# Joining the two words of a 64-bit weight on VectorE instead of ScalarE and GpSimd

## The chip, the cores and the metric

The kernel runs on one core of one Trainium2 chip. A core has five engines, each with its own instruction queue: TensorE (PE in the profile; its weight loads are shown apart as PEld), VectorE (DVE), ScalarE (ACT), GpSimd (POOL) and SyncE (SP), which here issues most of the transfers. Work on different engines is ordered by semaphores only. The metric is the time of one execution on the device, in microseconds (us). Before the change its median is 1007.48 us (three runs, 1007.32 to 1007.81).

## The reference

Attention with a causal window and a linear position bias, then a bilinear feed-forward layer:

```
q, k, v: (8, 8, 576, 64) float32
w_a, w_b: (512, 1536) float64;  w_out: (1536, 512) float64

scores = q @ k^T / 8 - slope[h] * |i - j|    where 0 <= i - j < 128, else -1e9
x      = softmax(scores) @ v                 -> (4608, 512)
out    = ((x @ w_a) * (x @ w_b)) @ w_out     -> (4608, 512)
```

The weights arrive as 64-bit floating-point numbers. The kernel has to turn them into 32-bit ones itself, and then into pairs of 16-bit ones (a high and a low part), since the products run in float16 with three terms each.

## The kernel before, in words

There are eight batches. For each, an attention stage makes x (512 rows by 576 tokens), an "up" stage makes the product of two projections (1536 rows, in 12 blocks f), and a "down" stage multiplies it with w_out. While PE works on one batch's up and down stages, the attention of the next batch runs beside it in small steps.

The weights are prepared once, beside batch 0. `up_weights` goes through 12 blocks of w_a and w_b, `down_weights` through 6 pairs of blocks of w_out: 18 conversions in all, each of 128 x 1024 values that lie as pairs of 32-bit words (low, high) in a buffer which is a part of the tile `wdn`. Three such buffers take turns. The result, float32, goes to a part of the tile `wup`. One conversion (`convert`) is:

- L131, DVE: the high word shifted left by 3 and masked: the exponent's low bits and the upper 20 bits of the mantissa at their float32 place.
- L133, DVE: the two top bits of the high word (sign and exponent) joined to it.
- L130, ACT: the low word, read as an unsigned number, times 2^-29, written back as an integer: the 3 mantissa bits that are still missing.
- L135, POOL, twice (each for 512 of the 1024): that number added.

Behind it ACT squares the converted block into a free place (L141), PE sums the squares with a matrix of ones (L156, tile `wn_ps`; for w_out an accumulated sum and, at the end, L101), DVE takes the largest (L161), POOL makes a power of two from it (L107, L111, L114), and with that scale ACT (L149) writes the float16 high part and DVE (L150) the low part into `wup`. For w_out this last step is L230 and L231, into `wdn`.

The attention of batch 0 (`first_attention`) is the first thing that PE does. For each of four head pairs and four banks of scores PE makes products (L569, `sc_ps`), DVE adds the bias and takes the minimum (L580, `mn`), ACT the exponential (L581), PE transposes (L587), DVE or ACT copies (L592 to L595), and at the end of a pair PE multiplies with v (L501, `x_ps`) and DVE scales (L619). Steps of the weights are put between: `other(0.5)` twice per bank. Then comes batch 0's up stage (L836, tile `up_ps`, evacuated by ACT at L783 and DVE at L785, split into float16 parts at L829 and L830, the latter on DVE for the first six blocks and on POOL for the last six), with batch 1's attention beside it (L374, L382, L383, L399, L400, L296), and its down stage (L812).

What sets the order: SP's queue is in the order of the code throughout, and PE's from batch 1 on. All other queues, and PE's through batch 0, are ordered at build time by a scheduler that works with its own durations. The loads of weights (L119) stand in SP's queue: the load for conversion n+3 is issued behind the sum of squares of conversion n. In SP's queue before the load for the ninth conversion stands the load of v for batch 1 (L268).

Of the kernel before, what the change touches and what calls it, by code (L numbers as in the profile page):

```python
# [15 lines left out]
U32 = mybir.dt.uint32  # L16
I64 = mybir.dt.int64
AF = mybir.ActivationFunctionType
ALU = mybir.AluOpType
# [27 lines left out]
def attention_then_bilinear_ffn(ctx: ExitStack, tc: tile.TileContext, qT, kT, vP, w_a, w_b, w_out, rel, slopes2, outT):  # L47
    nc = tc.nc
    vec, act, pe, pool, sp = nc.vector, nc.scalar, nc.tensor, nc.gpsimd, nc.sync
# [71 lines left out]
    def words(n):  # L121

        w = raws[n % 3].bitcast(I32).rearrange("p m (n two) -> p m n two", two=2)
        return w[:, :, :, 0], w[:, :, :, 1], forms[n % len(forms)].bitcast(I32)

    def convert(n):

        low, high, t = words(n)

        act.activation(low, low.bitcast(U32), AF.Copy, scale=float(2.0**-29))  # L130
        vec.tensor_scalar(out=t, in0=high, scalar1=3, scalar2=0x3FFFFFF8, op0=ALU.logical_shift_left, op1=ALU.bitwise_and)  # L131
        yield
        vec.scalar_tensor_tensor(out=t, in0=high, scalar=-0x40000000, in1=t, op0=ALU.bitwise_and, op1=ALU.bitwise_or)  # L133
        for m in range(2):
            pool.tensor_tensor(out=t[:, m, :], in0=t[:, m, :], in1=low[:, m, :], op=ALU.add)  # L135
        yield

    def squares(n, **kw):
# [26 lines left out]
    def up_weights():  # L165
# [3 lines left out]
        sq, rest, hi, ps = {}, [], [], None  # L169
        for f in range(NF + 2):  # L170
            conv = convert(f) if f < NF else iter(())
            next(conv, None)
            n = f - 1
# [30 lines left out]
    def down_weights():  # L204

        sums = small.tile([P, NF // 2], F32, tag="wos", name="wos", bufs=1)
        for n in range(NF // 2 + 1):
            conv = convert(NF + n) if n < NF // 2 else iter(())
            next(conv, None)
            yield  # L210
            next(conv, None)
            if n:
                squares(NF + n - 1, accum_out=sums[:, n - 1:n])
                if n + 2 < NF // 2:
                    load_weights(NF + n + 2, (w_out[2 * n + 4], w_out[2 * n + 5]), sp)
            yield
        sab = small.tile([P, NF], F32, tag="sab", name="sab", bufs=1)
        vec.tensor_tensor(out=sab, in0=sup[:, :, 0], in1=sup[:, :, 1], op=ALU.mult)
        vec.tensor_reduce(out=smin, in_=sab, op=ALU.min, axis=AX)
        vec.reciprocal(sab, sab)  # L220
        s1 = small.tile([P, 1], F32, tag="wo1", name="wo1", bufs=1)
        vec.tensor_reduce(out=s1, in_=sums, op=ALU.add, axis=AX)
        tot = ps_at.tile([P, 512], F32, tag="at", name="wtot")
        total(tot[:, 0:1], s1)
        power_scale(so, tot[:, 0:1], 1.01, 15)
        vec.tensor_scalar(out=ratio, in0=sab, scalar1=smin, scalar2=so, op0=ALU.mult, op1=ALU.mult)
        yield
        for f in range(NF):
            s, x = ratio[:, f:f + 1], forms[f // 2][:, f % 2, :]
            act.activation(wdn[:, f, 0, :], x, AF.Copy, scale=s)  # L230
            vec.scalar_tensor_tensor(out=wdn[:, f, 1, :], in0=x, scalar=s, in1=wdn[:, f, 0, :], op0=ALU.mult, op1=ALU.subtract)  # L231
            yield
# [828 lines left out]
```

## Time and profile before

| | us |
|---|---|
| median of three runs | 1007.48 |
| span of the profiled execution, first to last instruction | 1005.2 |
| PE busy | 970.8 (97%) |
| DVE busy | 674.8 (67%) |
| ACT busy | 648.9 (65%) |
| POOL busy | 306.1 (30%) |
| L130, 18 on ACT | 20.9 |
| L131, 18 on DVE | 15.9 |
| L133, 18 on DVE | 24.1 |
| L135, 36 on POOL | 54.6 |

The profile is one execution; of it the span is known, which begins with the first instruction of the program and ends with the last, and the run's own time lies a little above it, as the median of the runs does (2.3 us). Busy time is time in which an engine executes; a matmul's end is modelled, so a busy PE is not PE at its peak. In a group's row the figure behind the bar is its busy time, the next the mean duration in ns, and then follows how long the engine was idle just before these instructions and what ended that. All 18 conversions lie in the first 153 us.

### The profile page before, as it was taken

How to read it: one execution, taken by the hardware profiler on the slowest of the kernel's cores; microseconds unless marked ns; L12 is line 12 of the kernel's file. 1: busy time of each engine (PE TensorE's matmuls, PEld its weight loads, DVE VectorE, ACT ScalarE, POOL GpSimd, SP SyncE). 2: the span in 40 equal slices, each digit the busy share in tenths (PEclk: the TensorE clock that was granted, in tenths of full speed). 3: DMA queues.
4: the chain of work that ended last, by engine and by line, in shares of the span. 5: the costliest groups of instructions: out<-in, count | busy, mean ns of one | idle time of the engine just before them, and what ended most of it. 6: DMA issues, size and time to landing. Idle time of an engine off the chain costs nothing.

```text
span 1005.2 us, 23888 instructions
## 1 busy us (share of the span) xinstructions
PE 970.8 (97%) x9339; PEld 753.6 (75%) x9339; DVE 674.8 (67%) x1833; ACT 648.9 (65%) x1715; POOL 306.1 (30%) x345
## 2 busy tenths in 40 slices
PE   8789989999999999999999999999999999999998
PEld 5557656777777777777787777777777777777776
DVE  5888999557878566785768687666677576524530
ACT  7976779657767756767767767677666766413321
POOL 3533463104565321352226112220223022211100
PEclk9889999999999999999999999999999999999999
DMA  9317733564444442462624642474425632210001
GB/s 349 120 43 269 231 114 74 120 166 80 100 90 100 137 90 43 97 172 71 121 52 105 172 90 46 93 178 103 84 57 107 163 67 43 49 37 7 2 13 36
DMA packets 148433, 102.83 MB, mean 102 GB/s; under 512 B 120032, under 2 KB 128352, under 8 KB 147296
## 3 DMA queue, kind: packets, MB, share of 16 engines
q1 hardware_dynamic: 138816, 91.77, 37.2%
q10 hardware_dynamic: 9504, 9.54, 2.9%
q8 instruction: 73, 1.20, 0.5%
q14 instruction: 40, 0.33, 0.1%
HBM read 48.33 MB, written 9.44 MB: 57 GB/s over the span
## 4 chain that ended last, share of the span: by engine, by line
PE 70%; DVE 10%; ACT 4%; DMA 2%; issue 1%; POOL 1%; SPq 0%; ACTq 0%; DVEq 0%
PE dn_ps L932 19%; PE ch L836 19%; PE p L836 14%; PE up_ps L836 10%; PE x_ps L501 4%; PE sc_ps L378 3%; DVE phl L400 2%; PE dn_ps L812 2%; DMA v<-in_vP 1%; DVE t L382 1%; DVE xs L436 1%; ACT t L383 1%; DVE wup L150 1%; ACT phl L399 1%; DVE wup L257 1%
## 5 line engine op out<-in xcount | busy, mean ns | idle before, releaser
L836 PEld LDWEIGHTS <-wup 128*128 128x128 f16 x4224 | 409.1, 98 | 120.8 <-issue 14.3
L932 PE MATMUL dn_ps<-h,wdn 128*128 128x288 f16 x2016 | 254.3, 286 | 0.0
L932 PEld LDWEIGHTS <-wdn 128*128 128x128 f16 x2016 | 193.9, 98 | 51.7
L836 PE MATMUL ch<-xs,wup 128*128 128x288 f16 x1536 | 221.5, 286 | 0.8 <-ACT rc L861 0.6
L836 PE MATMUL up_ps<-xs,wup 128*128 128x288 f16 x1536 | 197.7, 288 | 5.8 <-DVE rc L785 4.2
L836 PE MATMUL p<-xs,wup 128*128 128x288 f16 x1152 | 172.6, 286 | 0.0
L891 POOL TENSOR_TENSOR rc<-rc,row 128x288 f32<-128x288 f32 x64 | 62.3, 974 | 278.8 <-DVE row L889 262.9
L400 DVE SCALAR_TENSOR_TENSOR phl<-t,rin,phl 128x192 f16<-128x192 f32 (+2 forms) x252 | 109.5, 474 | 19.0 <-ACT phl L399 18.8
L383 ACT ACTIVATE t<-t,mn 128x192 f32<-128x192 f32 (+2 forms) x252 | 107.2, 427 | 23.3 <-DVE mn L382 23.0
L829 ACT CAST h<-rc 128x576 f16<-128x576 f32 x96 | 64.2, 669 | 68.2 <-DVE rc L896 37.6
L399 ACT ACTIVATE phl<-t,rin 128x192 f16<-128x192 f32 (+2 forms) x252 | 88.7, 425 | 23.0 <-DMA pT<-phl 10.9
L830 DVE TENSOR_TENSOR h<-rc,h 128x576 f16<-128x576 f32 x90 | 71.1, 790 | 32.7 <-ACT h L829 32.0
L382 DVE CUSTOM_DVE_ANT_0 t<-sc_ps,bias,neg 128x192 f32<-128x192 f32 (+2 forms) x216 | 73.7, 389 | 7.8 <-PE sc_ps L378 7.7
L135 POOL TENSOR_TENSOR wup<-wup,wdn 128x512 int32<-128x512 int32 x36 | 54.6, 1539 | 44.6 <-DVE wup L133 14.6
L937 ACT ACTIVATE row<-dn_ps,oi 128x288 f32<-128x288 f32 x56 | 27.6, 494 | 56.7 <-PE dn_ps L932 56.5
L873 ACT ACTIVATE row<-ch,g 128x288 f32<-128x288 f32 x64 | 31.8, 497 | 50.1 <-PE ch L836 50.1
L436 DVE TENSOR_TENSOR xs<-v,xs 128x576 f16<-128x576 f32 x52 | 48.7, 950 | 21.7 <-ACT xs L435 21.5
L360 POOL TENSOR_SCALAR bias<-rel_sb,ninv,sl_sb 128x192 f32<-128x192 f32 x24 | 21.3, 887 | 123.5 <-DVE mn L382 123.5
L868 DVE TENSOR_TENSOR rc<-p,rc 128x288 f32<-128x288 f32 x64 | 29.1, 454 | 44.4 <-PE p L836 35.0
L896 DVE SCALAR_TENSOR_TENSOR rc<-rc,g,ch 128x288 f32<-128x288 f32 x64 | 32.6, 510 | 23.8 <-PE ch L836 23.6
L383 ACT ACTIVATION_READ_ACCUMULATOR t<-t,mn 128x1 f32 x252 | 47.7, 189 | 0.0
L430 POOL TENSOR_TENSOR xq<-xq,sq 128x576 bf16<-128x576 bf16 x22 | 29.6, 1345 | 56.8 <-ACT sq L429 56.7
(151 smaller groups left out, 1315.6 us busy)
## 6 DMA issues: line engine op xcount, KB each, us to landing
v<-in_vP SPq DMA_DIRECT2D x8, 1280.0 KB, 6.5
out<-row ACTq DMA_DIRECT2D x60, 144.0 KB, 1.8
qk<-in_qT SPq DMA_DIRECT2D x28, 288.0 KB, 3.9
qk<-in_kT SPq DMA_DIRECT2D x28, 288.0 KB, 4.4
wdn<-in_w_a SPq DMA_DIRECT2D x12, 512.0 KB, 4.5
wdn<-in_w_b SPq DMA_DIRECT2D x12, 512.0 KB, 5.6
wdn<-in_w_out SPq DMA_DIRECT2D x12, 512.0 KB, 4.3
qst<-qkh SPq DMA_DIRECT2D x24, 144.0 KB, 2.7
```

The costliest lines, as they stand in the source:

```text
L135: pool.tensor_tensor(out=t[:, m, :], in0=t[:, m, :], in1=low[:, m, :], op=ALU.add)
L382: vec.tensor_tensor_reduce(out=t[:, c:c + w], in0=ps[:, c:c + w], in1=o.bias[:, WIN - w:WIN], scale=-0.125 if o.b == 1 else o.neg, scalar= ...
L383: act.activation(t[:, c:c + w], t[:, c:c + w], AF.Exp, bias=o.mn[:, n:n + 1], scale=-1.0, accum_out=o.sm[:, n:n + 1])
L399: act.activation(phl[:, 0, pc:pc + w], e, AF.Copy, scale=s)
L400: vec.scalar_tensor_tensor(out=phl[:, 1, pc:pc + w], in0=e, scalar=s, in1=phl[:, 0, pc:pc + w], op0=ALU.mult, op1=ALU.subtract)
L436: vec.tensor_tensor(out=xs[:, n, 1, :, :], in0=src, in1=xs[:, n, 0, :, :], op=ALU.subtract)
L501: pe.matmul(xp[oc // 512][64 * h:64 * h + 64, o0:o0 + w], vt[0:rows, c:c + 64], probs(pt, rows, blocks, h), start=(n == 0 and first), stop ...
L829: act.copy(h[:, f, :, 0, :], hid)
L830: eng.tensor_tensor(out=h[:, f, :, 1, :], in0=hid, in1=h[:, f, :, 0, :], op=ALU.subtract)
L836: pe.matmul(ps[:, 0:HT], wup[:, a[0], a[1], wi, k, :], xs[:, b, xi, k, :], start=(first and n == 0), stop=(last and n == len(ks) - 1), ski ...
L891: pool.tensor_tensor(out=x0, in0=x0, in1=mid, op=ALU.mult)
L932: pe.matmul(ps[:, 0:HT], wdn[:, f, wi, e * P:(e + 1) * P], h[:, f, t, hi, :], start=(m == 0 and n == 0), stop=(m == NF - 1 and n == 2))
```

## The change

The ACT conversion of the low word and the two POOL additions go. In their place DVE takes the low word, shifts it right by 29, so that its three top bits remain, and joins it with the rest by a bitwise or, one instruction over all 1024 values:

```diff
         low, high, t = words(n)
 
-        act.activation(low, low.bitcast(U32), AF.Copy, scale=float(2.0**-29))
         vec.tensor_scalar(out=t, in0=high, scalar1=3, scalar2=0x3FFFFFF8, op0=ALU.logical_shift_left, op1=ALU.bitwise_and)
         yield
         vec.scalar_tensor_tensor(out=t, in0=high, scalar=-0x40000000, in1=t, op0=ALU.bitwise_and, op1=ALU.bitwise_or)
-        for m in range(2):
-            pool.tensor_tensor(out=t[:, m, :], in0=t[:, m, :], in1=low[:, m, :], op=ALU.add)
+        vec.scalar_tensor_tensor(out=t.bitcast(U32), in0=low.bitcast(U32), scalar=29, in1=t.bitcast(U32), op0=ALU.logical_shift_right, op1=ALU.bitwise_or)
         yield
```

Lines behind the edit have numbers lower by two in the changed kernel; in it the shift is L130, the joining of the top bits L132 and the new join L133.

The scheduler orders the queues of batch 0 anew. The differences end with batch 0's down stage; behind it every queue is as before, and SP's is throughout. Three places show it. The first is DVE in batch 0's attention, third head pair, from behind its third bank of scores to the first of the next pair. Before:

```order
L133 SCALAR_TENSOR_TENSOR wup<-wdn,wup 128x2x512
L150 SCALAR_TENSOR_TENSOR wup<-wup,sup 128x2x256 x3
L131 TENSOR_SCALAR wup<-wdn 128x2x512
L150 SCALAR_TENSOR_TENSOR wup<-wup,sup 128x2x256
L580 ISA t,mn_546<-sc_ps,bias_331 128x192
L580 ISA mn_546 128x1
L580 ISA t,mn_546<-sc_ps,bias_331 128x192
L580 ISA mn_546 128x1
L595 COPY phl<-tr_ps 128x512
L133 SCALAR_TENSOR_TENSOR wup<-wdn,wup 128x2x512
L580 ISA t_163,mn_578<-sc_ps,bias_483 128x64
```

After (L132 is the former L133, L133 the join, L578 the former L580):

```order
L132 SCALAR_TENSOR_TENSOR wup<-wdn,wup 128x2x512
L133 SCALAR_TENSOR_TENSOR wup<-wdn,wup 128x2x512
L578 ISA t,mn_538<-sc_ps,bias_327 128x192
L578 ISA mn_538 128x1
L578 ISA t,mn_538<-sc_ps,bias_327 128x192
L578 ISA mn_538 128x1
L130 TENSOR_SCALAR wup<-wdn 128x2x512
L133 SCALAR_TENSOR_TENSOR wup<-wdn,wup 128x2x512
L593 COPY phl<-tr_ps 128x512
L132 SCALAR_TENSOR_TENSOR wup<-wdn,wup 128x2x512
L601 TENSOR_SCALAR rin_605<-sm_426 128x9
L133 SCALAR_TENSOR_TENSOR wup<-wdn,wup 128x2x512
```

The four splits of weights (L150) that stood between the third and fourth bank stand earlier now; two conversions' steps and their joins stand there and behind the fourth bank.

The second place is DVE in batch 0's up stage, around the last splits of w_a and w_b and two evacuations. Before:

```order
L785 SCALAR_TENSOR_TENSOR rc<-rc,g,up_ps 128x288
L219 TENSOR_REDUCE smin<-sab 128x1
L150 SCALAR_TENSOR_TENSOR wup<-wup,sup 128x2x256
L133 SCALAR_TENSOR_TENSOR wup<-wdn,wup 128x2x512
L150 SCALAR_TENSOR_TENSOR wup<-wup,sup 128x2x256 x2
L220 RECIPROCAL sab<-sab 128x12
L150 SCALAR_TENSOR_TENSOR wup<-wup,sup 128x2x256
L392 TENSOR_SCALAR rin<-sm 128x4
L785 SCALAR_TENSOR_TENSOR rc<-rc,g,up_ps 128x288
```

After (L148 is the former L150, L783 the former L785, L828 the former L830):

```order
L133 SCALAR_TENSOR_TENSOR wup<-wdn,wup 128x2x512
L148 SCALAR_TENSOR_TENSOR wup<-wup,sup 128x2x256 x3
L217 TENSOR_REDUCE smin<-sab 128x1
L132 SCALAR_TENSOR_TENSOR wup<-wdn,wup 128x2x512
L783 SCALAR_TENSOR_TENSOR rc<-rc,g,up_ps 128x288
L828 TENSOR_TENSOR h<-rc,h 128x2x288
L783 SCALAR_TENSOR_TENSOR rc<-rc,g,up_ps 128x288
L390 TENSOR_SCALAR rin<-sm 128x4
```

A join stands ahead of the splits, and the evacuations follow more closely on each other.

The third place is POOL at the end of the conversions. Before:

```order
L135 TENSOR_TENSOR wup<-wup,wdn 128x512 x2
L830 TENSOR_TENSOR h<-rc,h 128x2x288
L135 TENSOR_TENSOR wup<-wup,wdn 128x512 x4
L830 TENSOR_TENSOR h<-rc,h 128x2x288
L135 TENSOR_TENSOR wup<-wup,wdn 128x512 x2
L830 TENSOR_TENSOR h<-rc,h 128x2x288
```

After:

```order
L107 TENSOR_SCALAR cl<-wtop 128x4
L111 TENSOR_SCALAR r<-cl 128x4
L114 TENSOR_SCALAR sup<-r 128x4
L358 TENSOR_SCALAR bias<-rel_sb,sl_sb 128x192
L828 TENSOR_TENSOR h<-rc,h 128x2x288 x4
```

POOL keeps the scales, the biases and its share of the low parts of the hidden layer (L828), without an addition between them.

## Prediction

> **What bounds the kernel now.** I read the page's head first, then a table of stretches, then who made TensorE (PE) wait.
>
> ```profile
> PE 970.8 (97%) x9339; PEld 753.6 (75%) x9339; DVE 674.8 (67%) x1833; ACT 648.9 (65%) x1715; POOL 306.1 (30%) x345
> PEclk9889999999999999999999999999999999999999
> ```
>
> PE is busy 97% of the span, so an edit elsewhere pays only where it shortens one of PE's gaps or a spell of low clock. The table of stretches tells where those are (columns: stretch, its length, busy time of PE, PEld, DVE, ACT, POOL, then the granted clock, the DMA share and GB/s):
>
> ```profile
> 0.00:20.00 20.00, 15.68 (x172) 12.24 (x173) 9.63 (x31) 13.20 (x35) 7.06 (x25) 0.91 0.92 353
> 20.00:54.00 34.00, 26.74 (x266) 17.56 (x263) 30.84 (x87) 32.19 (x87) 17.05 (x19) 0.90 0.46 169
> 54.00:86.00 32.00, 28.07 (x262) 20.78 (x262) 24.96 (x63) 23.44 (x59) 10.44 (x16) 0.89 0.30 113
> 86.00:158.00 72.00, 63.76 (x536) 46.73 (x534) 68.55 (x128) 53.50 (x118) 40.74 (x31) 0.95 0.57 178
> 215.00:1005.20 790.20, 781.47 (x7538) 614.59 (x7537) 501.12 (x1407) 485.86 (x1311) 220.85 (x248) 1.00 0.37 85
> ```
>
> From 215 us on PE idles 8.7 us in 790, at full clock. Before 158 us it idles 23.8 us (4.3 + 7.3 + 3.9 + 8.2). All 18 weight conversions lie there: eight before 86 us, ten between 86 and 158. In the last stretch VectorE (DVE) is busy 68.55 of 72 us. It is the bound there; PE follows it. From 20 to 54 us DVE (30.84 of 34) and ACT (32.19) are both nearly full. PE's waits between 86 and 160 us, and the largest two before, agree:
>
> ```profile
> PE up_ps L836 <- DVE rc L785: 4.2, 2, 2.3
> PE wtot L101 <- ACT t L383: 1.7, 1, 1.7
> PE wn_ps L156 <- ACT wdn L141: 1.5, 1, 1.5
> PE sc_ps L374 <- DVE mn L382: 0.7, 1, 0.7
> ...
> PE sc_ps L569 <- DVE mn L580: 4.2, 2, 4.0
> PE wn_ps L156 <- DVE mn L382: 3.1, 1, 3.1
> ```
>
> Why is DVE so full? The groups of DVE and POOL from 86 to 158 us (count, busy, mean ns), with the two pieces of the timeline that explain the means, and the durations over the whole span (min/median/max):
>
> ```profile
> L150 DVE SCALAR_TENSOR_TENSOR wup<-wup,sup 128x512 f16<-128x512 f32 x11 | 14.0, 1289 | 1.0 <-ACT wup L149 1.0
> L133 DVE SCALAR_TENSOR_TENSOR wup<-wdn,wup 128x1024 int32<-128x1024 int32 x10 | 13.7, 1381 | 0.0
> L131 DVE TENSOR_SCALAR wup<-wdn 128x1024 int32<-128x1024 int32 x10 | 9.4, 938 | 0.2 <-DMA wdn<-in_w_b 0.2
> L830 DVE TENSOR_TENSOR h<-rc,h 128x576 f16<-128x576 f32 x5 | 5.8, 1157 | 1.3 <-ACT h L829 1.3
> L296 DVE SCALAR_TENSOR_TENSOR vhl<-v,sv,vhl 128x640 f16<-128x640 f32 x3 | 5.7, 1922 | 1.5 <-ACT vhl L295 1.5
> L135 POOL TENSOR_TENSOR wup<-wup,wdn 128x512 int32<-128x512 int32 x20 | 31.1, 1579 | 27.1 <-DVE wup L133 9.6 <-ACT wdn L130 8.1 <-ACT vhl L295 4.2
> ```
> ```profile
> 109.27 2.98 POOL L135 TENSOR_TENSOR wup<-wup,wdn 128x512 int32<-128x512 int32 x2 [3.72 <-ACT wdn L130]
> 109.35 3.44 DVE L150 SCALAR_TENSOR_TENSOR wup<-wup,sup 128x512 f16<-128x512 f32 x2
> ```
> ```profile
> L150 DVE SCALAR_TENSOR_TENSOR wup<-wup,sup x24: 733/746/1783, 33.7 to 131.6; 128x512 f16<-128x512 f32 x24
> L133 DVE SCALAR_TENSOR_TENSOR wup<-wdn,wup x18: 1203/1218/2206, 9.3 to 146.8; 128x1024 int32<-128x1024 int32 x18
> L131 DVE TENSOR_SCALAR wup<-wdn x18: 631/686/1778, 8.1 to 141.5; 128x1024 int32<-128x1024 int32 x18
> L130 ACT ACTIVATE wdn<-wdn x18: 1111/1157/1211, 8.1 to 140.5; 128x1024 int32<-128x1024 uint32 x18
> L830 DVE TENSOR_TENSOR h<-rc,h x6: 741/754/1841, 81.1 to 125.1; 128x576 f16<-128x576 f32 x6
> L296 DVE SCALAR_TENSOR_TENSOR vhl<-v,sv,vhl x4: 879/1908/1948, 142.7 to 170.4; 128x640 f16<-128x640 f32 x4
> ```
>
> Two L150 that take 0.75 us each elsewhere took 3.44 us together because POOL's two additions started 0.08 us earlier: each DVE operation lost about 1 us. That is the hidden price of the additions: they occupy POOL, which has time, and block DVE, which has none.
>
> **What the change adds.** One join per conversion, in the shape of L133 (128x1024, one strided and one packed int32 operand). The trace has no join; its nearest row is L133, at 1.22 us. The bounds are L131's 0.69 and L133 under POOL, 2.2; I take L133, which has the same operands. On the queue it is worth its step from start to start: L133 began at 107.00 and the L150 behind it at 108.14, so 1.14 us.
>
> ```profile
> 107.00 1.22 DVE L133 SCALAR_TENSOR_TENSOR wup<-wdn,wup 128x1024 int32<-128x1024 int32 x1
> 108.14 0.75 DVE L150 SCALAR_TENSOR_TENSOR wup<-wup,sup 128x512 f16<-128x512 f32 x1
> ```
>
> Ten joins from 86 to 158 us: +11.4. Eight before: +9.1. The join waits for no other engine, only for DVE's own L133 line before it and the load that L131 needed anyway. Queued behind it are L150, the score reductions L382 and the evacuations L785, for which PE waits.
>
> **What it removes from DVE.** Mean less median (for L296 less its minimum), times the count, from 86 to 158 us: L150 11 x 0.543 = 6.0; L133 10 x 0.163 = 1.6; L131 10 x 0.252 = 2.5; L830 5 x 0.403 = 2.0; L296 3 x 1.043 = 3.1. Sum 15.2 us. What the probability splits of L400 lose besides, I set against what POOL's own L830, which stays, will still take. Net on DVE there: 11.4 - 15.2 = **-3.8 us**. Bounds: -7 if L400's share counts too, and 0 if the remaining POOL work takes back a quarter of the 15.2.
>
> **What it removes elsewhere.** ACT loses 18 x 1.16 = 20.9 us of L130 and POOL 36 additions. In the saturated stretch ACT is busy 53.5 of 72 us, so this alone buys nothing; what counts is the chain from shift to square: join 1.2 in place of a POOL pair of 2.5 to 3.0 that often started late. The last conversion shows it:
>
> ```profile
> 146.76 1.89 DVE L133 SCALAR_TENSOR_TENSOR wup<-wdn,wup 128x1024 int32<-128x1024 int32 x1
> 149.75 2.54 POOL L135 TENSOR_TENSOR wup<-wup,wdn 128x512 int32<-128x512 int32 x2
> 152.32 1.06 ACT L141 ACTIVATE wdn<-wup 128x1024 bf16<-128x1024 f32 x1 [0.50 <-POOL wup L135]
> ```
>
> From the end of L133 (148.65) to the square 3.7 us pass; with a join it is 1.2. PE's waits on these squares, 1.7 (through the sum at L101) and 1.5, can shrink by up to 2.5 each; but DVE would then be the next to be late, so of these 3.2 us I count **-1.0** beyond the DVE sum (bounds 0 and -3.2).
>
> **Before 86 us.** The same rows there:
>
> ```profile
> L150 DVE SCALAR_TENSOR_TENSOR wup<-wup,sup 128x512 f16<-128x512 f32 x13 | 12.9, 1031 | 0.0
> L133 DVE SCALAR_TENSOR_TENSOR wup<-wdn,wup 128x1024 int32<-128x1024 int32 x6 | 8.0, 1326 | 0.0
> L131 DVE TENSOR_SCALAR wup<-wdn 128x1024 int32<-128x1024 int32 x6 | 5.1, 858 | 0.0
> ```
>
> Stalls: 13 x 0.285 + 6 x 0.108 + 6 x 0.172 = 5.4 us, less than the 9.1 of the joins: DVE gets 3.7 us more, ACT 8 x 1.16 = 9.3 less. DVE has 3.2 us idle from 20 to 54 and 7.0 from 54 to 86 to take it, and ACT, just as full, gets faster. The order fits: between the last two score banks of a head pair stand six operations now (one L133, four L150, one L131, the block behind PE's 4.0 us wait) and two after, but more joins follow behind the last bank. I count **0**, with bounds -3 and +4.
>
> **The clock.** Long gaps cost PE twice. The same kind of 28 products:
>
> ```profile
> 55.24 2.12 PE L501 MATMUL x_ps<-phl,v 128*64 128x128 f32 x28
> ...
> 65.93 1.03 PE L156 MATMUL wn_ps<-wdn,ones 128*128 128x256 bf16 x4 [3.13 <-DVE mn L382]
> 66.89 3.88 PE L501 MATMUL x_ps<-pT,v 128*64 128x128 f32 x28
> ```
>
> After 3.13 us idle they took 1.8 us more. From 86 to 158 us the clock was 0.95 of full, 3.6 us' worth; with half of the gaps gone I count **-1.2** (bounds 0 and -3.6). The Trainium skill ("TensorE: Matmul & The Clock Gate", Part 1) has a free-running window of about 3.4 us, after an idle one of which the clock halves. By it every gap below 3.4 us would be free and this term nearly 0; the trace has the slow products behind a shorter gap, so I keep the term.
>
> **Sum.** -3.8 - 1.0 + 0 - 1.2 = -6.0 us. The profiled span is 1005.2, 2.3 below the median of the runs, 1007.48; span 999.2, time **1001.5**. From 215 us on PE is the bound and the instruction order is the same, so I carry the gain to the end whole.
>
> **The rivals.**
> 1. *More than this* (0.14). The first part gains as well: ACT was as full as DVE from 20 to 54 us, and the gaps of 4.0 and 3.1 us with their cold products go. Another -3 to -8: 990 to 998. Against it: DVE's own load rises there.
> 2. *Nothing to measure* (0.18). The lock stays under another name: POOL's L830 and its small scale operations are still there, and a DVE queue packed with two-input operations holds POOL up, and so L149 and L150 behind it; or the order, made anew by the scheduler, gives the 6 us back in new gaps. 1005.5 to 1009.5.
> 3. *DVE becomes the bound of the first attention; slower* (0.20). From 20 to 54 us the new order puts six more bit operations, two more L150 and one more reduction ahead of the last score bank: 6 x 1.14 + 2 x 0.67 + 0.6 = 8.8 us. The stalls that go there are in these rows, 4.15 - 3 x 0.67 and 1.78 - 0.69, together 3.2:
>
> ```profile
> 33.67 4.15 DVE L150 SCALAR_TENSOR_TENSOR wup<-wup,sup 128x512 f16<-128x512 f32 x3
> 37.74 1.78 DVE L131 TENSOR_SCALAR wup<-wdn 128x1024 int32<-128x1024 int32 x1
> ```
>
> 30.84 + 8.8 - 3.2 = 36.4 in a stretch of 34. If DVE's 3.2 us idle stay as well, the last scores come 5.6 us late, and a gap beyond 3 us adds some 2 to 3 us of cold products: +8, against -6 behind it, +2; and if the second stretch gives nothing, +8. 1009.5 to 1015.5. It is decided where the last L580 ends: in the trace near 53.8 us; beyond about 58 the change loses.
>
> The Trainium skill ("Perfetto Trace Analysis", Optimizing Scalar/DVE Operations) advises to take work off a saturated DVE to ScalarE or GpSimd, the reverse of this change, and adds that DVE and GpSimd share a port; the stalled L150 rows bear out the second half, so I give the first no more than this chance.
>
> **Chances.** Forecast case 0.48 (998.5 to 1005); rivals as above. Faster by over 0.2% (2 us, about what a measurement here can tell from no change): 0.48 + 0.14 = 0.62; within: 0.18; slower: 0.20. The range that leaves out no more than 2 in 10 is 993 to 1012: the far ends of rivals 1 and 3 are cut.
>
> **What would show it.** Right: L150, L131 and L296 at their short durations (means near 0.75, 0.69, 0.9 us); joins at 1.2 us; PE's idle time from 86 to 158 us down from 8.2 to about 4; POOL without L135. Wrong: DVE means that stay long over L830; a last L580 well behind 54 us; or a new wait of PE on L141 behind the join. If DVE's stalls go but PE's gaps stay, the gaps were the order's and not DVE's load.

## The result, and the profile after

The changed kernel takes 1010.38 us (median of seven runs, 1008.78 to 1011.34), the kernel before beside it 1007.53 us (seven runs, 1006.31 to 1008.81). The ratio is 1.0026, with a 95% interval of 1.0016 to 1.0036: slower by 1.6 to 3.6 us, where 6 us less were forecast. The time lies in the range of the prediction, the direction does not.

The head of the changed kernel's page, and its table of stretches (length, busy time of PE, PEld, DVE, ACT, POOL, granted clock, DMA share, GB/s):

```profile
PE 970.9 (96%) x9339; PEld 752.5 (75%) x9339; DVE 669.1 (66%) x1851; ACT 630.7 (63%) x1697; POOL 258.1 (26%) x309
PEclk8989999999999999999999999999999999999999
```
```profile
0.00:20.00 20.00, 15.01 (x152) 11.98 (x154) 9.30 (x29) 11.04 (x33) 3.27 (x21) 0.83 0.89 341
20.00:54.00 34.00, 27.73 (x283) 17.13 (x283) 32.79 (x92) 26.95 (x79) 7.43 (x10) 0.95 0.49 176
54.00:86.00 32.00, 26.50 (x248) 19.12 (x248) 22.77 (x65) 19.86 (x55) 4.66 (x12) 0.89 0.20 74
86.00:158.00 72.00, 67.49 (x623) 51.37 (x621) 64.50 (x141) 46.91 (x115) 13.48 (x12) 1.00 0.63 195
158.00:215.00 57.00, 50.41 (x473) 36.47 (x471) 36.90 (x111) 37.34 (x101) 8.59 (x7) 0.97 0.47 96
215.00:1008.10 793.10, 783.78 (x7572) 616.42 (x7571) 502.86 (x1418) 488.56 (x1319) 220.70 (x248) 1.00 0.38 86
```

The row of the kernel before that the prediction's table did not have:

```profile
158.00:215.00 57.00, 55.10 (x572) 41.68 (x570) 39.70 (x123) 40.69 (x112) 9.96 (x9) 1.00 0.51 108
```

From 86 to 158 us PE is idle 4.5 us where it was 8.2, at clock 1.00 (of full speed) where it was 0.95. From 158 to 215 us it is the reverse: 6.6 us idle where it was 1.9, at 0.97 where it was 1.00. So the time was won, and lost again in the next stretch. The rows of batch 0's up products, first those of the kernel before, then those of the changed one (count, duration, start of the first and the last), show how much was won by then:

```profile
L836 PE MATMUL up_ps<-xs,wup x576: 282/286/448, 57.6 to 168.5; 128*128 128x288 f16 x192
```
```profile
L834 PE MATMUL up_ps<-xs,wup x576: 282/286/448, 61.1 to 163.0; 128*128 128x288 f16 x192
```

The first of them is 3.5 us later, the last 5.5 us earlier, so between the two PE won 9.0 us. DVE's groups in the changed kernel from 86 to 158 us:

```profile
L132 DVE SCALAR_TENSOR_TENSOR wup<-wdn,wup 128x1024 int32<-128x1024 int32 x10 | 12.7, 1269 | 0.0
L133 DVE SCALAR_TENSOR_TENSOR wup<-wdn,wup 128x1024 uint32<-128x1024 uint32 x10 | 12.2, 1215 | 0.0
L148 DVE SCALAR_TENSOR_TENSOR wup<-wup,sup 128x512 f16<-128x512 f32 x11 | 8.0, 759 | 0.4 <-ACT wup L147 0.4
L130 DVE TENSOR_SCALAR wup<-wdn 128x1024 int32<-128x1024 int32 x10 | 7.1, 717 | 0.0
L828 DVE TENSOR_TENSOR h<-rc,h 128x576 f16<-128x576 f32 x6 | 4.5, 750 | 2.1 <-ACT h L827 2.1
L294 DVE SCALAR_TENSOR_TENSOR vhl<-v,sv,vhl 128x640 f16<-128x640 f32 x3 | 2.7, 920 | 0.7 <-ACT vhl L293 0.7
```

The long means that the prediction named are short now (L148 is the former L150: 1289 to 759 ns), and the join costs 1.215 us.

Now the stretch in which it was lost: who made PE wait from 158 to 215 us, first in the kernel before, then in the changed one (total, times, longest):

```profile
PE n_ps L515 <- ACT row L822: 1.1, 1, 1.1
PE up_ps L836 <- ACT rc L783: 0.5, 1, 0.5
```
```profile
PE x_ps L499 <- DMA pT<-phl: 4.3, 2, 3.3
PE qtot L330 <- DVE both L322: 1.7, 2, 1.0
PE dn_ps L810 <- ACT row L820: 0.4, 1, 0.4
PE dn_ps L810 <- DVE row L818: 0.3, 1, 0.3
```

The new wait is for a transfer, the transpose of the probabilities pT<-phl of batch 1's attention, which is issued by SP once ACT and DVE have written all of phl (the normalisation, L397 and L398). There is one per head pair; the fourth lies here. SP's row of it before and after (start, length of the issue):

```profile
185.59 5.57 SPq L405 DMA_TRANSPOSE pT<-phl  x1
```
```profile
192.25 6.08 SPq L403 DMA_TRANSPOSE pT<-phl  x1
```

ACT's queue tells why it is 6.7 us late. Before, the pair's last four normalisations and then the squares of the next q and k, which wait for their load:

```profile
183.58 1.49 ACT L399 ACTIVATE phl<-t,rin 128x192 f16<-128x192 f32 x4 [0.45 <-DVE rin L396]
189.03 1.16 ACT L321 ACTIVATE qkl<-qk 128x1152 bf16<-128x1152 f32 x1 [3.96 <-DMA qk<-in_kT]
```

After, the same two the other way round:

```profile
188.69 1.16 ACT L319 ACTIVATE qkl<-qk 128x1152 bf16<-128x1152 f32 x1 [3.91 <-DMA qk<-in_kT]
189.76 0.19 ACT L319 ACTIVATION_READ_ACCUMULATOR qkl<-qk 128x1 f32 x1
189.85 1.48 ACT L397 ACTIVATE phl<-t,rin 128x192 f16<-128x192 f32 x4
```

The load lands within 0.4 us of the same time in both. In the changed kernel ACT sits idle 3.91 us in front of it, and behind it stand four normalisations, whose factors (`rin`) DVE had ready at 185.50 us. The transpose then also takes longer from issue to landing, 9.4 us instead of 7.6. And PE, at the end of this chain, in the changed kernel:

```profile
201.69 1.71 PE L499 MATMUL x_ps<-pT,vhl 128*64 128x128 f16 x42 [3.33 <-DMA pT<-phl]
203.34 1.14 PE L810 MATMUL dn_ps<-h,wdn 128*128 128x288 f16 x4
```

### The profile page after: what moved, and what is told of

The parts are those of the page before. It is cut to its first block, busy times and chain, and to the rows that moved or that the text cites. A ratio compares the mean times of both kernels' runs of the same rounds, so it can differ in the third digit from the quotient of the medians.

```text
span 1008.1 us, 23824 instructions
## 1 busy us (share of the span) xinstructions
PE 970.9 (96%) x9339; PEld 752.5 (75%) x9339; DVE 669.1 (66%) x1851; ACT 630.7 (63%) x1697; POOL 258.1 (26%) x309
## 4 chain that ended last, share of the span: by engine, by line
PE 69%; DVE 14%; DMA 7%; ACT 5%; issue 2%; SPq 1%; POOL 1%; ACTq 0%; DVEq 0%
PE dn_ps L930 19%; PE ch L834 18%; PE p L834 13%; PE up_ps L834 11%; PE x_ps L499 4%; PE sc_ps L376 3%; DMA pT<-phl 3%; DVE phl L398 2%; DMA qk<-in_kT 2%; DVE t L380 1%; DVE wup L133 1%; DMA v<-in_vP 1%; DVE wup L132 1%; DVE wup L148 1%; DMA qst<-qkl 1%
## 5 line engine op out<-in xcount | busy, mean ns | idle before, releaser
L834 PE MATMUL up_ps<-xs,wup 128*128 128x288 f16 x1536 | 195.5, 287 | 2.5 <-DVE wup L133 1.2
L398 DVE SCALAR_TENSOR_TENSOR phl<-t,rin,phl 128x192 f16<-128x192 f32 (+2 forms) x252 | 107.8, 467 | 27.1 <-ACT phl L397 27.0
L397 ACT ACTIVATE phl<-t,rin 128x192 f16<-128x192 f32 (+2 forms) x252 | 88.8, 425 | 34.3 <-DMA pT<-phl 21.1
L828 DVE TENSOR_TENSOR h<-rc,h 128x576 f16<-128x576 f32 x90 | 69.2, 769 | 33.6 <-ACT h L827 32.8
L499 PE MATMUL x_ps<-pT,vhl 128*64 128x128 f16 (+3 forms) x1176 | 46.2, 229 | 6.5 <-DMA pT<-phl 5.2
L499 PEld LDWEIGHTS <-vhl 128*64 128x64 f16 (+1 forms) x1176 | 42.7, 109 | 12.1 <-issue 5.8
```

The source lines that it names most:

```text
L397: act.activation(phl[:, 0, pc:pc + w], e, AF.Copy, scale=s)
L398: vec.scalar_tensor_tensor(out=phl[:, 1, pc:pc + w], in0=e, scalar=s, in1=phl[:, 0, pc:pc + w], op0=ALU.mult, op1=ALU.subtract)
L499: pe.matmul(xp[oc // 512][64 * h:64 * h + 64, o0:o0 + w], vt[0:rows, c:c + 64], probs(pt, rows, blocks, h), start=(n == 0 and first), stop ...
L828: eng.tensor_tensor(out=h[:, f, :, 1, :], in0=hid, in1=h[:, f, :, 0, :], op=ALU.subtract)
L834: pe.matmul(ps[:, 0:HT], wup[:, a[0], a[1], wi, k, :], xs[:, b, xi, k, :], start=(first and n == 0), stop=(last and n == len(ks) - 1), ski ...
```

## The experiments

In the diffs below, which are cut to the lines that matter, `tc.issue_after(x)` puts an instruction behind x in the order made at build time.

Theory A: the joins and the freed engines win some 6 us up to 158 us, and the order that the scheduler made anew loses more than that behind it, through late transposes. Rivals: B, the joins' time on DVE is what the change costs, and the order nothing; C, batch 1's transposes and loads have a fixed length and can't keep up with an earlier PE, however they are ordered; D, which came up with experiment 3, an order that helps does so whatever converts the weights. Every ratio is to the kernel before, run on the same chip in the same turn.

**1. The squares put back behind the normalisation.** In the changed kernel:

```diff
+        with tc.issue_after(last_norm[3].ins) if (b, p) == (2, 1) else ExitStack():
             act.activation(lo.bitcast(BF16), qk, AF.Square, accum_out=sums)
```

`last_norm[p]` is the last L397 of pair p. In the kernel before, the squares stand there already.

> The changed kernel with one place of ScalarE's order put back: the squares of the second q, k pair of batch 2 (which wait for its load) stand behind the last normalisation of batch 1's fourth pair, as they stand in the kernel before, not ahead of it. Theory A (the gain up to 158 us is real, and the new order behind it loses it, this transpose above all): the fourth transpose pT<-phl, issued at 192.25 us in the changed kernel, is issued near 187 us and lands near 195; the PE wait of 3.33 us at 201.69 us goes, and with it the clock dip to .66 of full speed behind it; the time falls by 3 to 4.5 us from the changed kernel's, to 1006 to 1007.5 us, ratio to the kernel before .9985 to 1.000. Rival B (the joins' load on VectorE costs the time, the order nothing): no change, ratio 1.0026. Rival C (the transposes and loads of batch 1's attention have a fixed length and cannot keep up with a PE that comes earlier, however they are ordered): the wait moves to the next transpose or load, and less than 1 us is won, ratio 1.0016 to 1.0026.

Measured: 1.0014 (1.0004 to 1.0023). That is 1.2 parts in 1000 below the changed kernel, no clear difference, and outside what theory A expected. The fourth transpose is issued at 188.87 us, 3.4 us earlier, not the 5 expected; PE is at the place earlier too and still waits 3.0 us. The edit moved other instructions as well: DVE's splits of phl (L399) now have five score reductions among them and end at 188.80 us, and the transpose takes 9.7 us to land. So the swap was not the only cause of the late transpose.

**2. The swap alone, in the kernel before.** `last_sq[0]` is the last of the squares.

```diff
+            if i == 3:
+                early = squares(5)
             if o:
-                with behind():
+                with tc.issue_after(last_sq[0].ins) if i == 3 else behind():
                     normalize(o)
...
-                nxt = squares(i + 1)
+                nxt = early if i == 4 else squares(i + 1)
```

> The kernel before, with the additions on GpSimd as they were, and the same swap made in it: the squares of the second q, k pair of batch 2 stand ahead of the last normalisation of batch 1's fourth pair on ScalarE; nothing else in any engine's order moves but the small product that follows them on VectorE. Theory A: ScalarE waits for the load until near 189 us with the normalisation behind it, the fourth transpose is issued near 191 us and not at 185.59, lands near 199, and PE, which wants it at 196.9, waits 2 to 3 us there: 1.5 to 3.5 us slower, ratio 1.0015 to 1.0035, with no join in the kernel. Rival B: nothing, ratio within .0005 of 1. Rival C: PE is not early in this kernel, so the transpose has slack: under 1 us, ratio below 1.001.

Measured: 1.0058 (1.0046 to 1.0070), twice what was expected. No join is in this kernel, and by the trace one instruction moved on ACT (with the read of its sum) and one on DVE, every other queue being as before; so rival B's "the order costs nothing" has fallen. The transpose is issued at 191.03 us. PE before, and then here:

```profile
196.86 1.63 PE L501 MATMUL x_ps<-pT,vhl 128*64 128x128 f16 x42
198.42 3.12 PE L812 MATMUL dn_ps<-h,wdn 128*128 128x288 f16 x24
```
```profile
200.74 2.91 PE L501 MATMUL x_ps<-pT,vhl 128*64 128x128 f16 x42 [3.29 <-DMA pT<-phl]
203.58 4.53 PE L815 MATMUL dn_ps<-h,wdn 128*128 128x288 f16 x24
```

The wait is 3.29 us, a little over the 2 to 3 expected; the same 66 products then take 7.44 us, not 4.75. The low clock behind the wait, which the expectation had left out, is 2.7 of the 5.8 us.

**3. The third transpose too.** Its normalisation stood, in the changed kernel, behind four splits of w_out and three exponentials:

```profile
166.81 2.56 ACT L228 ACTIVATE wdn<-wup,ratio 128x512 f16<-128x512 f32 x4
...
170.71 0.79 ACT L397 ACTIVATE phl<-t,rin 128x192 f16<-128x192 f32 x2
```

Experiment 1's edit, and beside it:

```diff
+            with tc.issue_after(last_norm[2].ins) if f >= 8 else ExitStack():
                 act.activation(wdn[:, f, 0, :], x, AF.Copy, scale=s)
```

> The first of these kernels, and beside that the last four splits of the output weights (f from 8) put behind the normalisation of batch 1's third pair on ScalarE. Theory A: the third transpose, issued at 174.04 us in the changed kernel, is issued about 2 us earlier, and the PE wait of .94 us at 180.89 goes: .5 to 1.5 us below the first of these kernels. Against it: the last splits come later, and the first down products, which read them in order, may wait up to 2 us for them. Rivals B and C: no difference to the changed kernel of more than 1 us.

Measured: 0.9958 (0.9946 to 0.9970), 6.8 parts in 1000 below the changed kernel where 3.5 to 6 were expected of both edits together. ACT now, and the stretch:

```profile
167.65 0.81 ACT L399 ACTIVATE phl<-t,rin 128x192 f16<-128x192 f32 x2
168.35 1.33 ACT L229 ACTIVATE wdn<-wup,ratio 128x512 f16<-128x512 f32 x2
```
```profile
158.00:215.00 57.00, 52.86 (x523) 39.50 (x521) 40.73 (x136) 40.58 (x114) 7.51 (x7) 1.00 0.57 123
```

The third transpose is issued 4.5 us earlier (169.57 us), the fourth at 183.05, because phl must be free of one before it can be written for the next: ACT's first write for the fourth pair waits for the third transpose, in the changed kernel and here:

```profile
180.86 1.68 ACT L397 ACTIVATE phl<-t,rin 128x64 f16<-128x64 f32 x5 [4.17 <-DMA pT<-phl]
```
```profile
176.38 1.68 ACT L399 ACTIVATE phl<-t,rin 128x64 f16<-128x64 f32 x5 [0.85 <-DMA pT<-phl]
```

The long PE wait is gone and the clock is 1.00. Both edits seem to be needed: the squares back alone (experiment 1) won nothing clear, and with the splits late but the squares first (experiment 8) nothing is won either. No run has the edit of the splits alone.

**4. No joins at all.** The line of the join is taken out of the changed kernel; all 18 go (the ten of the expectation are those from 86 us on), and this kernel leaves out the low three bits of each weight.

> The changed kernel without the ten joins on VectorE: the low three bits of each weight are left out, so VectorE loses 18 operations of 1.22 us (22 us), and GpSimd has no additions either; the order behind is the scheduler's for this case. Rival B (the joins' time on VectorE is what the change costs): at least 3 us below the changed kernel, 1007 us or less. Theory A: PE is 1 to 6 us further ahead at 158 us, since 12 of the 22 us lie in 86 to 158 us, where VectorE is the busiest engine of the two that feed PE; its order in 158 to 215 us still has squares ahead of the fourth pair's normalisation, so 3 us or more are lost there, and the end comes out within 2 us of the changed kernel's. Rival C: the same end as the changed kernel within 1 us, because what is gained before 158 us is waited away behind it.

Measured: 0.9856 (0.9844 to 0.9869), 17 us below the changed kernel. Theory A's "within 2 us" missed by far, and rival C has fallen: PE came to the last up product at 150.2 us, 12.8 us earlier than in the changed kernel, and kept it all. The joins are a real cost on PE's path, as rival B says (the queues of batch 0 are ordered anew here too, so the 17 us have the order's share in them); what they are set against is experiment 6.

**5. The control: experiment 3's edits in the kernel before.**

> The control for the run that won: the kernel before, with its additions on GpSimd, and the same two edits of order in it (the last four splits of the output weights behind the normalisation of batch 1's third pair; the squares edit moves nothing there). Theory A (the edit gives back what the change had lost behind 158 us): PE waits for no transpose in the kernel before, so nothing is to be won; within 2 us of the kernel before, ratio .998 to 1.002. Rival D (the edit is an improvement of its own, whatever converts the weights): 3 us or more faster, ratio .997 or less, and then the change itself is no gain even with its order mended.

Measured: 1.0004 (0.9995 to 1.0012). The third transpose is 3.6 us earlier there as well (166.91 us), and nothing is won, since PE did not wait for it. D has fallen: what experiment 3 gains is what the change had lost.

**6. No additions, and no joins.** From the kernel before only the two additions go, in all 18 conversions; this kernel, too, leaves out the low three bits:

```diff
-        for m in range(2):
-            pool.tensor_tensor(out=t[:, m, :], in0=t[:, m, :], in1=low[:, m, :], op=ALU.add)
```

> The kernel before without the twenty additions on GpSimd, its conversions on ScalarE left as they are, and no join on VectorE: the low three bits of each weight are left out. It tells the lock's price from the joins': the additions held VectorE up for 21 to 26 us before 160 us in the kernel before. Theory A: VectorE's stalls go, the first down product, at 169.5 us in the kernel before and 151.2 in the changed kernel without joins, comes at 151 to 157 us, and the end is 8 to 14 us faster than the kernel before, less what the new order loses in 158 to 215 us. Rival B as it now stands (the joins cost on PE's path nearly what the lock cost, one for one): the same, and the difference to the changed kernel is the joins' 18 x 1.22 = 22 us less the conversions' cost. If the lock was mostly hidden beside ScalarE: less than 5 us faster.

Measured: 0.9850 (0.9837 to 0.9863), 15 us. The stretches from 86 us on:

```profile
86.00:158.00 72.00, 71.81 (x661) 53.62 (x660) 62.40 (x158) 64.26 (x143) 10.20 (x13) 1.00 0.56 168
158.00:215.00 57.00, 55.18 (x551) 42.91 (x550) 34.72 (x120) 36.70 (x112) 9.99 (x10) 1.00 0.64 147
```

PE has no gap left to speak of, though ACT still converts. So the additions are worth 15 us. That this is their hold on DVE, and not the shorter chain from shift to square or the new order, is argued from the stalls and not shown by a run of its own. The conversions on ACT are worth nothing by the end (experiment 4, without them, ends at the same time), but not on the way there: without them the last up product comes 4.2 us earlier (150.2 us), and batch 0's down stage then takes 3.6 us longer (50.3 us, 46.7 here). The changed kernel, with the join and without the conversion, is behind this one by 8.6 us at the last up product (154.4 us here, 163.0 in the changed kernel) and by 17.7 at the end: the other 9 are batch 0's down stage and its late transposes.

**7. The first four pieces as before, fourteen joined**, on top of experiment 3:

```diff
+        if n < 4:
+            act.activation(low, low.bitcast(U32), AF.Copy, scale=float(2.0**-29))
...
+        if n < 4:
+            for m in range(2):
+                pool.tensor_tensor(out=t[:, m, :], in0=t[:, m, :], in1=low[:, m, :], op=ALU.add)
+        else:
             vec.scalar_tensor_tensor(out=t.bitcast(U32), in0=low.bitcast(U32), scalar=29, in1=t.bitcast(U32), op0=ALU.logical_shift_right, op1=ALU.bitwise_or)
```

> The version that won (joins on VectorE, the last four splits and one squares later), but the first four pieces of the up weights are converted as in the kernel before (ScalarE conversion, GpSimd additions), the other fourteen by the join. In the changed kernel the first up product comes at 61.1 us, in the kernel before at 57.6. If the joins beside the first attention cost that 3.5 us: first up product at 57 to 59 us, and 1 to 3.5 us below the version that won (ratio .993 to .995). If the additions of the first four pieces stall VectorE by as much as four joins take (4.9 us): no change within 1 us. Its order behind 158 us is the scheduler's for this case, so up to 3 us may be lost there again.

Measured: 0.9924 (0.9912 to 0.9935), 3.4 parts in 1000 below experiment 3, as expected, and the best of all that compute the whole. The first up product comes at 54.0 us, 6 us before that of experiment 3 and further than expected, so with these four pieces joined the first attention takes longer than with their additions. Whether the join's time does it or the order isn't separated: experiment 6, with neither, has its first up product at 59.3 us. By the last up product only 0.5 of the 6 us are left (161.4 us, 161.9 in experiment 3); most of what this kernel gains on experiment 3 comes behind it, in a down stage of 47.4 us instead of 49.8. One wait takes much of what is lost between the two:

```profile
133.85 0.37 PE L506 MATMUL x_ps<-pT,vhl 128*64 128x128 f16 x4 [4.64 <-ACT vhl L299]
```

**8. Experiment 3 with the squares first again.** The swap of experiment 2, made in the version of experiment 3.

> The version with the last four output-weight splits late (ratio .9958), and in it the squares of the second q, k pair of batch 2 put back ahead of the last normalisation of batch 1's fourth pair on ScalarE, as the changed kernel has them. It tells what this swap alone is worth when the third transpose is on time. Theory A: the normalisation waits for the load until 187 to 189 us, the fourth transpose, issued at 183.05 us in that version, is issued at 188 to 191, PE waits 3 us for it near 195 and runs at a lower clock behind it: 3 to 6 us slower than that version, ratio .999 to 1.002. If only the splits mattered: within 1 us of it, ratio .995 to .997.

Measured: 1.0043 (1.0031 to 1.0055), 8.5 parts in 1000 above experiment 3: the swap costs all of the gain and more, with the third transpose on time (168.72 us). It isn't the swap alone as in experiment 2: from 181 to 202 us some evacuations, exponentials and splits on ACT and DVE changed places too. ACT, then PE:

```profile
185.16 1.16 ACT L320 ACTIVATE qkl<-qk 128x1152 bf16<-128x1152 f32 x1 [5.71 <-DMA qk<-in_kT]
186.23 0.19 ACT L320 ACTIVATION_READ_ACCUMULATOR qkl<-qk 128x1 f32 x1
186.32 1.48 ACT L398 ACTIVATE phl<-t,rin 128x192 f16<-128x192 f32 x4
```
```profile
199.77 2.41 PE L500 MATMUL x_ps<-pT,vhl 128*64 128x128 f16 x42 [3.33 <-DMA pT<-phl]
```

Expected were 3 to 6 us, again too little: the clock of the whole stretch is 0.94.

**9. Experiment 7 with v's scale first on DVE**, for the 4.64 us wait:

```diff
     def v_scale(st):
+      with tc.high_priority(offset=PRIO) if not states.get(1) else ExitStack():
```

> The best version so far (first four pieces converted as before, fourteen joined; ratio .9924) with the small operations of v's scale put first on VectorE while the first up runs: in that version ScalarE's split of v waited 2.56 us for the scale and PE 4.64 us for the split at 133.85 us. Theory A (gains before 158 us are kept where the transposes are not delayed): the wait shrinks to 0 to 2 us, and 2 to 4 us are won, ratio .988 to .991. If it only moves the wait: within 1 us, .9915 to .9935.

Measured: 0.9936 (0.9922 to 0.9949), no difference to experiment 7 that can be told, where theory A expected 2 to 4 us. The wait shrank to 3.01 us only.

**10. The same in experiment 3.**

> The version with all joins and the order mended (ratio .9958), and v's scale put first on VectorE in the same way. PE did not wait for it there, so by itself it is worth nothing: but the scheduler makes another order of some fifty instructions on VectorE and ScalarE from it, the third pair's normalisation ahead of the splits among them. It tells how far such an order alone moves the end: by theory A within 2 us of that version, ratio .994 to .998, as long as no transpose is issued later than in it.

Measured: 0.9981 (0.9972 to 0.9989), 2.3 parts in 1000 above experiment 3 and just outside what was expected. The third and fourth transposes are no later than in experiment 3 (166.40 and 182.79 us), so theory A doesn't explain these 2 us.

All of it in one table (us). The columns are the start of batch 0's last up product, of the fourth transpose, of batch 1's first up product, and two differences: the transpose behind the last up product (the lag), and the length of batch 0's down stage, from the last up product to the next first. They are of one profiled execution each, while the runs of one kernel differ by some 4 us; the profiled run of experiment 7 was the slowest of its six.

| kernel | last up | 4th transpose | next up | lag | down stage | ratio |
|---|---|---|---|---|---|---|
| before | 168.5 | 185.6 | 215.1 | 17.1 | 46.6 | 1 |
| changed | 163.0 | 192.3 | 218.0 | 29.3 | 55.0 | 1.0026 |
| 1 squares back | 162.9 | 188.9 | 217.3 | 26.0 | 54.4 | 1.0014 |
| 2 swap in before | 167.8 | 191.0 | 221.8 | 23.2 | 54.0 | 1.0058 |
| 3 order mended | 161.9 | 183.1 | 211.7 | 21.2 | 49.8 | 0.9958 |
| 4 no joins | 150.2 | 170.6 | 200.5 | 20.4 | 50.3 | 0.9856 |
| 5 control | 167.5 | 185.0 | 215.7 | 17.5 | 48.2 | 1.0004 |
| 6 no additions | 154.4 | 172.5 | 201.1 | 18.1 | 46.7 | 0.9850 |
| 7 four old | 161.4 | 176.7 | 208.8 | 15.3 | 47.4 | 0.9924 |
| 8 swap in 3 | 161.0 | 189.4 | 218.9 | 28.4 | 57.9 | 1.0043 |
| 9 | 160.2 | 175.5 | 207.6 | 15.3 | 47.4 | 0.9936 |
| 10 | 161.9 | 182.8 | 212.4 | 20.9 | 50.5 | 0.9981 |

With a lag of 15 to 18 us the down stage takes 46.6 to 48.2 us, at 20 to 21 about 50, and from 23 on 54 to 58.

## Why the prediction was wrong, point by point

**DVE is the bound from 86 to 158 us, and the additions stall it: right, and well sized.** The stalls of five lines were put at 15.2 us; by their means in both kernels these lines took 14.2 us less for the same counts. The Trainium skill ("SBUF — State Buffer", "SBUF: two separate sides") has DVE and GpSimd take turns at a shared pair of ports, with a lock for a whole instruction; the rows agree, L148 at 759 ns without GpSimd's additions where L150 took 1289 beside them.

**The join at L133's 1.22 us: right**, 1.215. DVE's net was put at -3.8 us; its busy time there fell from 68.55 to 64.50, by 4.05, but with four more evacuations and one more split (L828) in the stretch, so the two figures do not measure the same.

**The squares about right, the clock too small.** PE's idle time from 86 to 158 us was to fall from 8.2 to about 4 and fell to 4.5; the clock was to give 1.2 us and gave all of its 0.05, the 3.6 us that the prediction had as its bound. From batch 0's first up product to its last PE took 101.9 us instead of 110.9, for the same 866 instructions: 5.4 us less idle, where 4.8 were forecast, and 3.6 us less busy, at a mean clock of 0.97 instead of 0.94.

**Before 86 us: nothing, with bounds of -3 and +4. It cost 3.5 us, and the sign was wrong.** The last score reduction starts at 56.3 us (53.4 before), the first up product is 3.5 us late, and experiment 7, with the first four pieces as they were, has it at 54.0. Rival 3 had the mechanism, though the point from which it decides, 58 us, was not reached. By the last up product PE is 5.5 us ahead, against the 6.0 of the sum. That the two agree is luck: 9.0 us were won where the sum had 6.0, and 3.5 lost where it had nothing.

**The gain carried to the end whole: this step failed.** It read: "From 215 us on PE is the bound and the instruction order is the same, so I carry the gain to the end whole." From 215 us on that holds: from batch 1's first up product to the end of the span both take 790.1 us. But the sum ended at 158 us, and 158 to 215 us, where every queue but SP's is ordered anew, had neither a row nor a term. It was worth +8.4 us (a down stage of 55.0 us instead of 46.6), more than the 5.5 us that PE was ahead. What stood ready for it in ACT's order, before the run, was an instruction that waits for a load, put ahead of the normalisation that a transpose waits for. Its price could have been estimated from the trace before: the squares ended 6.7 us behind the point at which the normalisation started (190.3 and 183.58 us), the transpose landed 3.7 us before PE came for it, which leaves a wait of 3 us, and such a wait has its products at a low clock besides. Shown by experiment 2 (the swap alone: 5.8 parts in 1000 slower, without a join), 8 (the swap and what moved with it: 8.5 parts), 3 (the order mended: 4.2 parts faster than before) and 5 (the same mending in the kernel before: nothing). In the changed kernel the swap is not all of it: the third transpose was late as well, and experiment 1, which undid the swap there, won nothing clear.

**Rival 2** did name "the order, made anew by the scheduler", but only as giving back the 6 us at most. An order can take more than the change brings.

**What stays open:** experiment 3's down stage still takes 3.2 us more than that of the kernel before, and experiment 10's 3.9. Idle time makes up a part (4.1 us from 158 to 215 us against 1.9); the rest wasn't tried. Open, too, is why the fourth transpose takes longer to land where it is issued late: 9.4 to 10.3 us in the changed kernel and experiments 1, 2 and 8, against 7.2 to 7.9 in the kernel before and experiments 3 and 5. This adds some 2 us to each of those waits.

## What to carry to other kernels

Where a scheduler makes the order anew, a change is not done where its own instructions end: take the difference of the queues to its last row, and price each instruction that waits for a transfer and now stands ahead of others, by its wait in the trace before and by the slack of whoever waits behind it. A gain off the critical path of the next stage is kept only if that stage's transfers come earlier too; the lag from PE's last product to the transfer's issue tells this sooner than busy times do. And where a change comes out against a sound local sum, mend the order before giving the change up: here that alone turned +0.3% into -0.4%, and with the first four pieces left as they were into -0.8%.

## What the runs showed of the hardware that was not expected

A wait of some 3 us can cost PE nearly twice its length: behind 3.29 us idle, 66 products took 2.7 us more (experiment 2). In the 8 us behind the wait the granted clock was 0.64 there and 0.79 in the changed kernel and in experiments 1 and 8, against 1.00 at this place in the kernel before, so the price of such a wait varies, by these clocks from 1.7 to 2.9 us (an estimate). The slow spell need not begin with the first product: in the changed kernel the 42 products right behind 3.33 us idle took 1.71 us, nearly full speed (1.63), and the next four took 1.14. The Trainium skill ("TensorE: Matmul & The Clock Gate", Part 1) explains a moving point of change by a window of about 3.4 us that runs freely; that a gap of 3.00 us is enough (experiment 1: the same 42 products took 2.36 us behind it) speaks for less than one whole idle window.

The ScalarE conversions, 20.9 us of ACT in the kernel before, cost nothing that is left at the end: experiments 4 and 6 differ by them and end within 0.6 parts in 1000, though the last up product comes 4.2 us earlier without them.
